# An attention and expert kernel with its first pair, its first plan and its hand-over in another order

## The chip, the cores and the metric

The kernel runs on one core of one Trainium2 chip. The metric is the device time of one execution in microseconds (us); lower is better. The engines are named as in the profile: PE (TensorE matmuls, PEld its weight loads), DVE (VectorE), ACT (ScalarE), POOL (GpSimd), SP (SyncE, which issues most DMAs). On-chip memory is SBUF; matmul results land in PSUM.

## The reference

Attention over 8 batches and 8 heads (sequence 576, head dimension 64), then a mixture of experts with one expert per token. All of it is float32.

```python
def _attn_ref(q, k, v):                       # 8, 8, 576, 64
    ...
    q_rot, k_rot = (rotate(q), rotate(k))     # rotary embedding by cos, sin of the position
    scores = scale * np.matmul(q_rot, k_rot.transpose(0, 1, 3, 2))
    scores = scores - np.max(scores, axis=-1, keepdims=True)
    attn = np.exp(scores)
    attn = attn / (np.sum(attn, axis=-1, keepdims=True) + 1e-09)
    return np.matmul(attn, v)

def _moe_ref(x, modality_id, w_gate, modality_bias, w1, w2):
    N, D, E, F = 4608, 512, 8, 1024           # tokens, width, experts, hidden
    logits = x @ w_gate + modality_bias[modality_id]
    e_idx = np.argmax(logits, axis=1)
    ...                                       # gate_w: the softmax value of that expert
    for e in range(E):
        mask = e_idx == e
        h = np.maximum(x[mask] @ w1[e], 0.0)
        out[mask] = gate_w[mask, None] * (h @ w2[e])
```

## The kernel before

**Attention.** The 64 heads are worked on as 32 pairs; pair n holds two heads of batch n // 4. One tile holds a pair's rotated queries and keys, 128 rows by 1216 columns. A step (called a part in the code) rotates such a tile: part 0 multiplies by the cosines (L230), part 1 by the sines (L232), part 2 adds (L234), part 3 copies the sum rounded to the matmul's type on ScalarE (`acopy`, shown as L221, `HL<-ST`: the "high" half) and part 4 subtracts to get the rest (L238, the "low" half). Two DMAs per pair (L246, `SW<-HL`) swap the two heads' rows. Parts 0, 1, 2 and 4 run on VectorE for pairs 0 and 1 and on GpSimd from pair 2 on. Pair 0's tile is done in three column ranges, `FIRST`, whose inputs and tables come by DMAs of their own (L154 to L156), each with all five parts before the next.

A pair's scores are made in nine units of 128 queries (L261), numbered 0 to 8; unit 8 holds the last 64 queries of both heads. Units go through a ring of three PSUM tiles. Each gets a minimum on VectorE (L270; the sign of the scores is turned) and an exponential on ScalarE with the row sums (L277). Then P is transposed on PE through the same ring (L283, six "fills": F0 to F3, FA, FB), each evacuated half by VectorE (L315) and half by ScalarE (L221, `PH<-ps`, `PD<-ps`). AV matmuls (L339) in two halves A and B, copies, transposes back and division (L373 to L390) follow, and the finished rows go to the array X in DRAM.

**Routing and plans.** After the last pair of a batch that batch's logits, chosen experts and ranks are worked out (`route`, thirteen steps), and five indirect DMAs from GpSimd's queue (`scatter`, L472) write its tokens' numbers and weights to a table, TAB, sorted by expert. A block is 256 tokens of one expert. The first plan (`plan(0)`) cuts 8 full blocks out of the first six batches, while the last two are still in attention; the second cuts the rest. A plan is a chain of operations on a single partition, rows of 8, 64 or 8 by 8 numbers. In `plan(0)` GpSimd does all but a shift (L492) and three reductions, which VectorE does.

**Expert blocks.** `m_plan` reads a block's expert and place into registers of SP; `m_ix` loads its two index lists from TAB; `m_gather` (L614) fetches its token rows by indirect DMAs, eight of them; `m_load1` and `m_load2` load the expert's weights into the staging tiles ST1 and ST2 (the same tiles that hold the attention's inputs and tables). The weights are split into a high part (ScalarE, L221, `W1H`, `W2H`) and a low part (VectorE, L218, `W1L`, `W2L`). `m_tr` (L655) transposes the gathered rows, `m_tre` splits them. `m_l1` is the first layer (L673), `m_l1e` its activation (L681, L682), `m_l2` the second (L690) with its scaled result `y` and the indirect DMA to the output (L694).

**What sets the order.** Every step of a pair has a key time in the table `KEYS`, in microseconds on a period of 14.438; step s of pair n stands at key(s) + 14.438 n. A second table, `AT`, gives the keys of routing, plans, scatters and of the first expert block. All are sorted by key and emitted in that order, and each engine works through its instructions in the order in which they were emitted; SP's DMAs keep theirs too. The work on the first expert block is keyed relative to pair 31, the last one, so that it lies among the last pairs' work; negative keys lie before that pair. When the last pair's step keys are used up, the attention's pools are closed, and only then are the tiles for the split second-layer weights opened.

## Time and profile before

| what | value |
|---|---|
| time, median of 3 runs | 974.46 us (974.25 to 976.87) |
| the profiled execution's own time | 978.22 us |
| its span from first to last instruction | 976.4 us |
| PE busy | 908.2 us, 93% of the span |
| VectorE busy | 674.2 us, 69% |
| ScalarE busy | 632.3 us, 65% |
| GpSimd busy | 663.8 us, 68% |

Times inside the trace are counted from the start of the span. The program has three stretches: the start, until pair 0's scores run; 32 pairs of attention, a pair being counted from its first score matmul to that of the next; and the expert blocks to the end. In the view by windows each row is one stretch, with its length, then for PE, PEld, DVE, ACT and POOL the busy time and in brackets the number of instructions, then the clock that PE was granted (1.00 is full), the DMA engines' mean share and GB/s. In a timeline row stand start, duration, engine, line, operation, output and inputs, and in square brackets how long the engine had been idle and what released it. PE is the busiest engine, but in the start and around the hand-over to the experts it waits; these places are read by window and not from the shares above.

### The profile page before, as it was taken

The page shows a single profiled execution, that of the slowest core. Times are in us where ns is not written, and L with a number is a line of the kernel's source. Part 1 is how long each engine was busy: PE and PEld are TensorE (multiplying, and loading weights), DVE is VectorE, ACT ScalarE, POOL GpSimd, SP SyncE. Part 2 cuts the span into 40 slices and gives each one's busy share as a digit, 9 for nine tenths or more (in the row PEclk, how much of TensorE's full clock was granted, in tenths as well). Part 3 has the DMA queues.
Part 4 walks back from the last instruction along what each step waited for, and adds up shares of the span by engine and source line. Part 5 has one row for each costly group of instructions (what it writes and reads, how often), then busy time and mean ns, then how long its engine had stood idle before and what let it go on. Part 6 is the DMA issues. An engine that isn't in the chain of part 4 may idle for free. (4 is left out here: it accounts for less than half of the span.)

```text
span 976.4 us, 24969 instructions
## 1 busy us (share of the span) xinstructions
PE 908.2 (93%) x9248; PEld 742.4 (76%) x9248; DVE 674.2 (69%) x1158; ACT 632.3 (65%) x1299; POOL 663.8 (68%) x498
## 2 busy tenths in 40 slices
PE   1899999999999999989977899999999999999996
PEld 1677677777777767767646689999998888899995
DVE  6677777787777777777754478677666666666771
ACT  1778787787787877868753355666555656556661
POOL 7776788889878798799656076557666666556500
PEclk9799999999999999999989899999999999999998
DMA  9645667566574755746751261111431611611100
GB/s 285 194 142 173 180 198 221 148 188 202 174 225 134 201 185 175 228 130 182 207 149 34 64 211 36 55 48 58 142 120 42 218 38 45 227 44 49 41 24 15
DMA packets 71964, 132.71 MB, mean 136 GB/s; under 512 B 28395, under 2 KB 48267, under 8 KB 66844
## 3 DMA queue, kind: packets, MB, share of 16 engines
q1 hardware_dynamic: 61436, 110.32, 37.8%
q0 software_dynamic: 9536, 19.48, 6.4%
q8 instruction: 75, 1.23, 0.6%
q10 hardware_dynamic: 864, 1.25, 0.4%
q14 instruction: 53, 0.43, 0.2%
HBM read 140.59 MB, written 19.77 MB: 164 GB/s over the span
## 5 line engine op out<-in xcount | busy, mean ns | idle before, releaser
L270 DVE TENSOR_REDUCE mn<-ps 128x1 f32<-128x576 f32 x288 | 205.4, 744 | 104.2 <-PE ps L261 67.3
L277 ACT ACTIVATE P<-ps,mn 128x576 f32<-128x576 f32 x288 | 210.4, 737 | 97.6 <-DVE mn L270 90.4
L614 POOL DMA_INDIRECT XG<-X,iy x152 | 180.9, 1190 | 47.5 <-issue 41.4
L673 PE MATMUL psH<-HL,W1H 128*128 128x256 f32 x1152 | 202.7, 279 | 0.0
L261 PE MATMUL ps<-HL 64*128 64x288 f32 x960 | 170.7, 315 | 29.8 <-ACT HL L221 14.9
L261 PE MATMUL ps<-SW 64*128 64x288 f32 x960 | 170.3, 316 | 9.0 <-DMA SW<-HL 4.7
L261 PEld LDWEIGHTS ps<-HL 64*128 64x128 f32 x960 | 137.7, 190 | 53.2 <-ACT P L277 15.9
L673 PEld LDWEIGHTS psH<-HL,W1H 128*128 128x128 f32 x1152 | 176.8, 188 | 1.7
L673 PE MATMUL psH<-HL,W1L 128*128 128x256 f32 x576 | 160.8, 279 | 0.7 <-DVE W1L L218 0.7
L261 PEld LDWEIGHTS ps<-SW 64*128 64x128 f32 x960 | 135.4, 190 | 24.4 <-ACT P L277 14.1
L218 DVE TENSOR_TENSOR W1L<-ST,W1H 128x1024 fp32r<-128x1024 f32 x76 | 90.0, 1222 | 84.6 <-ACT W1H L221 82.6
L339 PE MATMUL pa<-PH,V 128*64 128x320 f32 (+1 forms) x1024 | 142.2, 420 | 1.1 <-PE ps L261 0.7
L694 POOL DMA_INDIRECT out_dram<-y,ix x38 | 39.1, 1030 | 143.6 <-ACT y L693 129.8
L690 PE MATMUL psY<-W2H,SW 128*128 128x512 f32 x304 | 120.3, 396 | 1.4 <-ACT W2H L221 1.4
L690 PE MATMUL psY<-W2L,SW 128*128 128x512 f32 x304 | 120.4, 396 | 0.4 <-DVE W2L L218 0.4
L283 PE MATMUL ps<-idf,P 64*128 64x64 f32 x2624 | 105.3, 229 | 8.8 <-DVE PH L315 2.4
L283 PEld LDWEIGHTS ps<-idf,P 64*128 64x128 f32 x2624 | 92.6, 141 | 22.7 <-ACT PH L221 8.6
L315 DVE COPY PH<-ps 128x512 f32<-128x512 f32 (+1 forms) x160 | 97.3, 632 | 17.4 <-PE ps L283 10.9
L339 PEld LDWEIGHTS pa<-PH,V 128*64 128x64 f32 x1024 | 69.8, 139 | 51.5 <-issue 14.5
L673 PEld LDWEIGHTS psH<-HL,W1L 128*128 128x128 f32 x576 | 108.2, 188 | 0.9 <-DVE W1L L218 0.9
L221 ACT ACTIVATE PH<-ps 128x512 f32<-128x512 f32 (+1 forms) x160 | 84.0, 556 | 22.1 <-PE ps L283 14.9
L218 DVE TENSOR_TENSOR W2L<-ST,W2H 128x1024 fp32r<-128x1024 f32 x76 | 92.4, 1220 | 4.1 <-ACT W2H L221 3.6
(159 smaller groups left out, 1602.9 us busy)
## 6 DMA issues: line engine op xcount, KB each, us to landing
ST<-in_moe_w_dram SPq DMA_DIRECT2D x152, 512.0 KB
ST<-in_qk_dram SPq DMA_DIRECT2D x31, 1216.0 KB
SW<-HL SPq DMA_DIRECT2D x124, 232.0 KB
V<-in_v_dram SPq DMA_DIRECT2D x64, 128.0 KB
X<-X SPq DMA_DIRECT2D x8, 1024.0 KB
XG<-X,iy POOLq DMA_INDIRECT x152
V<-in_v_dram SPq DMA_DIRECT2D x64, 16.0 KB
X<-XT SPq DMA_DIRECT2D x32, 32.0 KB
```

The lines of the kernel that those rows point to most:

```text
L218: nc.vector.tensor_tensor(o, a, b, op=ALU.subtract)
L221: return nc.scalar.activation(o, i, AF.Copy, scale=scale)
L261: free(nc.tensor.matmul(ps[:, g, 0:288], t[:, wq, q0:q0 + P], t[:, wk, k0:k0 + 288], start=(m == 0), stop=(m == len(L) - 1)), seen)
L270: lastmin[d["ring", u]] = nc.vector.tensor_reduce(mn, d["S", u][:, :, 0:288], op=ALU.min, axis=AX.XY).ins
L277: nc.scalar.activation(p.rearrange("p (a b) -> p a b", a=2), ps[:, :, 0:288], AF.Exp, bias=d.pop(("m", u)), scale=-1.0, accum_out=d["sum"] ...
L283: free(nc.tensor.transpose(ps[0][:, g, c:c + 64], src[r, k0:k0 + P], idf[r, r]), ps[1])
L315: mine.append((nc.vector.tensor_copy if g else acopy)(o, i).ins)
L339: nc.tensor.matmul(pa[hh * 64:hh * 64 + 64, 0:c1 - c0], d["V"][:, hh, kt, :], r, start=(kt == 0), stop=(kt == 4))
L614: nc.gpsimd.indirect_dma_start(out=XG[s % 2][:, t, g, :], out_offset=None, in_=X.rearrange("n (i f) -> (n i) f", f=P)[0:rows], in_offset=b ...
L673: nc.tensor.matmul(ps[:, i, :], w[:, c, f0:f0 + P], x[:, c, :], start=(m == 0), stop=(m == 11))
L690: nc.tensor.matmul(ps, hx[:, c, t * P:(t + 1) * P], w[:, c, :], start=(m == 0), stop=(m == 23))
L694: nc.gpsimd.indirect_dma_start(out=out, out_offset=bass.IndirectOffsetOnAxis(ap=d["ix"][:, t, 0:1], axis=0), in_=y, in_offset=None, bounds ...
```

## The change

1. **Pair 0.** The column ranges are other ones: 288 key columns, then 544 that hold the last query block and the other keys, then the 384 in between. The parts of the ranges are interleaved (a part of the next range stands before the low half of the one before). The load for pair 1 is issued after the second range's swap and no longer with the first inputs. The units of pair 0 come as 8, 6, 7, 0, 1 to 5 in the nine places of the key table; its evacuations stand right behind their fills, and both its AV halves right after the last fill.
2. **Pair 1.** Its parts 0, 1, 2 and 4 run on GpSimd instead of VectorE; its high copy and low half stand after pair 0's last fill. Parts 0 to 2 of pair 2 follow right behind it on GpSimd. The load for pair 3 and the seven GpSimd operations of `setup2` (routing constants) come later.
3. **First plan.** All 24 operations are on VectorE, spaced by 1.0 in the key table instead of 1.5. The scatters are spaced by 2.5 instead of 9.0 or 10.5; they, the first index copies and the last two batches' scatters are declared independent of each other, so none waits for another's write to TAB.
4. **First expert blocks.** Index copies, gathers, weight loads, the first layer's weight splits and the transposes have earlier keys: block 0's index copy at -45 instead of -16.5, its gathers from -41 to -15.8 instead of -12.5 to -3.4, block 1's from -13.5, block 2's from -3, the splits at -20, -15, -11, -4 instead of -14, -9, -5, -1, the transposes in pair 30 instead of pair 31.
5. **Second-layer weights.** Their high part takes the place in SBUF of the P tiles, their low part that of the transposed P, each as soon as the last reader in pair 31 is done; the splits get keys 10.2 to 20.5 within pair 31, and the first block's second layer stands 0.1 after the last pair's end instead of 2.0. The PSUM pools of the experts wait tile by tile.

```diff
 AT = dict(
-    pl=1.5,
-    sc=(10.5, 9.0),
...
+    pl=1.0,
+    sc=(2.5, 2.5),
...
-    FIRST = ((0, 416), (K1, QW), (416, K1))
+    FIRST = ((0, Q0), (672, QW), (Q0, 672))
...
     def rope_(n, part, c0=0, c1=QW):
         d = st[n]
-        e = nc.vector if n < 2 else nc.gpsimd
+        e = nc.vector if n < 1 else nc.gpsimd
...
+        for _b, x in placed:
+            tc.declare_no_dep(inst, x, reason="rows of other tokens")
...
     def plan(ph):
-
-        V_ = nc.vector if ph else nc.gpsimd
+        V_ = nc.vector
...
-    for n in range(2):
-        for c in FIRST if n == 0 else ((0, QW),):
-            for part in range(5):
-                rope_(n, part, *c)
-                if part > 2:
-                    swap(n, part - 3, *c)
-        load(n + 2)
+    for part, c in ((0, 0), (1, 0), (2, 0), (3, 0), (4, 0), (0, 1), (1, 1), (2, 1), (3, 1), (0, 2), (4, 1), (1, 2), (2, 2), (3, 2), (4, 2)):
+        rope_(0, part, *FIRST[c])
+        if part > 2:
+            swap(0, part - 3, *FIRST[c])
+        if (part, c) == (4, 1):
+            load(1)
+    load(2)
...
-    setup2()
+    for part in range(3):
+        rope_(1, part)
...
+    first = (8, 6, 7, 0, 1, 2, 3, 4, 5)
...
+    full = max(K[f] for f in K if f[0] in "SF") + 0.05
...
+    OV[0].update(AVA=full + 0.01, AVB=full + 0.02)
+    for i, nm in enumerate(("HI", "SWH", "LO", "SWL")):
+        OV[1][nm] = full + 0.03 * (i + 1) - PER
+    for i, nm in enumerate(("T1", "T2", "R")):
+        OV[2][nm] = full + 0.03 * (i + 5) - 2 * PER
+    J(full + 0.15, "load", 0, load, 3)
+    J(20.5, "setup2", 0, setup2)
...
+        if g == 0:
+            for i in range(2):
+                Z((A["hi2"], A["lo2"])[i][0] - 0.01, weights2, i)
+        Z(A["hi2"][g], m_hi, 1, g)
+        Z(A["lo2"][g], m_lo, 1, g)
...
-        Z(end + A["sp2"][g], m_split, 1, g)
     Z(end + A["l2"], m_l2, 0, 0)
...
     att.close()
-    mw = ctx.enter_context(tc.tile_pool(name="mw", bufs=1))
-    W2[0] = mw.tile([P, 8, DM], F32R, name="W2H")
-    W2[1] = mw.tile([P, 8, DM], F32R, name="W2L")
```

Three places show how the order moves. A row names line, operation, output, inputs and shape. The first is the end of pair 0 on ScalarE (HL0, HL1: rotated tiles of even and odd pairs; `re` and P4 to P3: the row sums of pair 0 and the exponentials of pair 1). Before:

```order
L221 ACTIVATE PD_115<-ps1_120 128x2x64
L221 ACTIVATE PH_114<-ps2_121 128x8x64
L221 ACTIVATE HL0_81<-ST1_73 128x1216
L354 ACTIVATE re_457<-sum_240,EPS_80 128x9
L277 ACTIVATE P4_113,sum_427<-ps0_119,mn_437 128x576
```

After:

```order
L234 ACTIVATE PD_113<-ps1_129 128x2x64
L234 ACTIVATE PH_127<-ps2_130 128x8x64
L234 ACTIVATE HL1_82<-ST2_74 128x1216
L234 ACTIVATE HL0_81<-ST1_73 128x1216
L367 ACTIVATE re_470<-sum_235,EPS_80 128x9
L290 ACTIVATE P4_112,sum_453<-ps0_128,mn_461 128x576
```

The high copy of pair 1 (HL1) now stands there too, and that of pair 2 (HL0) is still ahead of pair 1's first exponential. On GpSimd, after the DMA that clears TAB, the same place reads (ST1, ST2: inputs of even and odd pairs):

```order
L200 DMA TAB_64<-PH_114 128x648
L205 CAST MF_133<-MI_132 128x40
L209 TENSOR_TENSOR BI_134<-MF_133,MBB_135 128x320
L210 TENSOR_SCALAR MF_133<-MF_133 128x40
L211 TENSOR_TENSOR P0_109<-MF_133,MBB_135 128x320
```

and after the change:

```order
L213 DMA TAB_64<-PH_127 128x648
L243 TENSOR_TENSOR ST2_74<-ST2_74,ST1_73 128x1216
L245 TENSOR_TENSOR ST2_74<-ST2_74 128x1216
L247 TENSOR_TENSOR ST2_74<-ST2_74 128x1216
L251 TENSOR_TENSOR HL1_82<-ST2_74,HL1_82 128x1216
L243 TENSOR_TENSOR ST1_73<-ST1_73 128x1216
L245 TENSOR_TENSOR ST1_73<-ST1_73,ST2_74 128x1216
L247 TENSOR_TENSOR ST1_73<-ST1_73 128x1216
```

Between pair 1's high copy and pair 2's, ScalarE's rows above, GpSimd has pair 1's low half (L251) and pair 2's three parts (L243, L245, L247). The second place is VectorE in pair 26 (`mn`: a unit's minimum; `ni`, `nf`, `nb`, `t88`: the plan's rows). Before:

```order
L270 TENSOR_REDUCE mn_6964<-ps1_120 128x1
L270 TENSOR_REDUCE mn_6974<-ps2_121 128x1
L270 TENSOR_REDUCE mn_7000<-ps1_120 128x1
L492 TENSOR_SCALAR ni_6968<-ni_6968 1x8
L270 TENSOR_REDUCE mn_7014<-ps0_119 128x1
```

After:

```order
L283 TENSOR_REDUCE mn_6974<-ps1_129 128x1
L510 TENSOR_TENSOR nf_6979<-RUN_72,CF_70 1x8
L283 TENSOR_REDUCE mn_6984<-ps2_130 128x1
L512 TENSOR_SCALAR ni_6978<-nf_6979 1x8
L514 TENSOR_SCALAR ni_6978<-ni_6978 1x8
L283 TENSOR_REDUCE mn_7014<-ps1_129 128x1
L517 CAST nb_7027<-ni_6978 1x8
L283 TENSOR_REDUCE mn_7029<-ps0_128 128x1
```

Where one plan step stood between the minima there are now four, and so on through pairs 26 and 27. The third is VectorE's tail of the last pair (X, G, XT: finished attention rows and logits; HX: the first block's hidden layer). Before:

```order
L682 SCALAR_TENSOR_TENSOR HX_85<-ps1_120,SW0_83 128x512
L384 TENSOR_TENSOR X_7888<-pa_8957,ri_8918 128x8x32
L387 TENSOR_TENSOR G_139<-pa_8957,ri_8918 128x2x16
L218 TENSOR_TENSOR W2L_8980<-ST2_74,W2H_8979 128x1024 x4
L655 STREAM_TRANSPOSE XG1_76<-XG1_76 128x512 x2
```

After:

```order
L231 TENSOR_TENSOR W2L_8947<-ST2_74,W2H_8882 128x1024
L709 SCALAR_TENSOR_TENSOR HX_85<-ps1_129,SW0_83 128x512
L397 TENSOR_TENSOR X_8005<-pa_8987,ri_8949 128x8x32
L400 TENSOR_TENSOR G_147<-pa_8987,ri_8949 128x2x16
L682 STREAM_TRANSPOSE XG1_76<-XG1_76 128x512 x2
```

The four subtractions of the second layer's low weights no longer stand in a row behind the last pair's work but between its steps.

125 lines of the change are left out of this document (75 added, 50 removed).

## The prediction

> **What bounds the kernel now.** First the view by windows, edges at first score matmuls of pairs 0, 1, 2, 3, 26, 27, 28, 30, 31, at the first matmuls of the first expert block's two layers and of the second block, and at PE's end. Columns after the length: busy time and instructions of PE, PEld, DVE, ACT, POOL, PE's granted clock, DMA share, GB/s.
>
> ```profile
> 14.86:36.34 21.48, 13.48 (x142) 11.45 (x144) 15.83 (x19) 10.18 (x24) 17.67 (x11) 0.76 0.73 234
> 36.34:51.20 14.86, 14.49 (x209) 10.78 (x206) 10.54 (x22) 11.64 (x32) 10.44 (x4) 1.00 0.55 170
> 51.20:65.81 14.61, 14.45 (x209) 10.81 (x205) 10.90 (x24) 11.55 (x32) 10.96 (x6) 1.00 0.57 173
> 413.61:432.72 19.11, 15.91 (x209) 12.14 (x206) 14.04 (x27) 11.76 (x32) 15.99 (x16) 0.91 0.48 144
> 432.72:447.57 14.85, 14.64 (x203) 10.86 (x203) 11.14 (x26) 11.70 (x32) 13.59 (x17) 1.00 0.71 156
> 478.26:496.07 17.81, 15.27 (x210) 10.98 (x206) 13.27 (x26) 13.42 (x32) 7.12 (x7) 1.00 0.59 161
> 496.07:524.15 28.08, 19.35 (x203) 13.38 (x203) 17.22 (x30) 15.32 (x36) 17.11 (x17) 0.82 0.44 124
> 524.15:550.96 26.81, 21.55 (x158) 16.47 (x157) 5.63 (x17) 5.28 (x12) 10.31 (x11) 0.87 0.12 21
> 550.96:562.88 11.92, 11.53 (x48) 9.02 (x49) 8.91 (x11) 7.47 (x10) 1.02 (x1) 1.00 0.37 123
> 562.88:968.00 405.12, 403.89 (x2599) 363.95 (x2597) 275.29 (x316) 236.29 (x287) 231.21 (x193) 1.00 0.26 85
> ```
>
> An ordinary pair (third row) takes 14.61 us with PE busy for 14.45: PE sets its length, VectorE has 3.7 us to spare. So do the expert blocks from the second on (last row). The change touches neither; it touches the rows where PE is not full: pair 0, pair 26 (19.11 at a clock of 0.91), pair 31 and the first block.
>
> **The start.** Timeline rows of before, with the chain that sets pair 0:
>
> ```profile
> 10.03 0.46 DVE L238 TENSOR_TENSOR HL<-ST,HL 128x288 fp32r<-128x288 f32 x1 [0.51 <-ACT HL L221]
> 14.84 0.69 DVE L238 TENSOR_TENSOR HL<-ST,HL 128x512 fp32r<-128x512 f32 x1 [0.69 <-ACT HL L221]
> 18.42 0.60 PE L261 MATMUL ps<-SW 64*128 64x288 f32 x1 [2.96 <-DMA SW<-HL]
> 23.16 2.07 DVE L270 TENSOR_REDUCE mn<-ps 128x1 f32<-128x576 f32 x3
> 36.62 0.59 ACT L221 ACTIVATE PH<-ps 128x512 f32<-128x512 f32 x1
> 37.10 1.22 ACT L221 ACTIVATE HL<-ST 128x1216 fp32r<-128x1216 f32 x1
> 38.41 0.74 ACT L277 ACTIVATE P<-ps,mn 128x576 f32<-128x576 f32 x1
> ...
> L261 PE MATMUL ps<-HL 64*128 64x288 f32 x960 | 170.7, 315 | 29.8 <-ACT HL L221 14.9
> L261 PE MATMUL ps<-SW 64*128 64x288 f32 x960 | 170.3, 316 | 9.0 <-DMA SW<-HL 4.7
> ...
> L238 POOL TENSOR_TENSOR HL<-ST,HL 128x1216 fp32r<-128x1216 f32 x30 | 83.4, 2781 | 7.7 <-ACT HL L221 7.5
> ```
>
> The second row ends at 15.53, its swap lands 2.9 us later (18.42), and only then do the scores of pair 0 run on: unit 8 stands first and has its queries in the third range (its products of high halves start at 14.86, those with swapped rows wait). After the change, unit 8 has all its columns when two ranges are through. The second low half would then end near 11.85: 10.49 for its counterpart today, plus 1.4 for 256 more columns in each of four VectorE parts (0.69 for 512 in the second row, so 0.345 each). Scores run at 11.85 + 2.9 = 14.75, 3.7 us sooner. A unit costs PE 1.2 us ((170.7 + 170.3) / 288), so the third minimum, which ends at 25.23 today, can end 14.75 + 3 x 1.2 + 0.74 = 19.1: today VectorE does pair 1's four full-width parts in between, and these leave it. If the rest follows at today's pace, pair 0's last evacuation ends at 31.1 in place of 37.2: 6.1 gained.
>
> Then the new order takes it back. ScalarE does pair 1's high copy, 1.22, until 32.3; next in its order stands the high copy of pair 2, which needs pair 2's finished sum. GpSimd can begin pair 1's low half only when pair 1's high copy is done, and pair 2's three parts stand behind that low half. Four operations of 2.78 us are 11.1: ScalarE would stand until 43.4, copy until 44.6, and reach pair 1's first exponential at about 44.9 against 38.41 today. What queues behind it are all nine exponentials of pair 1; three units' scores can be made ahead, then the ring is full and PE waits too.
>
> From that exponential to pair 2's first scores go 12.8 us today (51.20 - 38.41). The AV of pair 0 is part of these; by the rows below it is 5.6 us of PE, and it would be done already. So pair 2 starts between 44.9 + 7.2 = 52.1 and 44.9 + 12.8 = 57.7, against 51.20. ScalarE has 10.4 us of pair 1's work left from there (11.64 in the second window row, less a high copy), which puts it at 55.3, and that I take: **+4**. Bounds: -6, if GpSimd's parts were done in the shade and all of the gain kept, and +7.
>
> ```profile
> L339 PE MATMUL pa<-PH,V 128*64 128x320 f32 x16 | 2.4, 439 | 0.0
> L339 PE MATMUL pa<-PH,V 128*64 128x256 f32 x16 | 1.9, 385 | 0.0
> L339 PE MATMUL pa<-PD,V 128*64 128x320 f32 x4 | 0.7, 432 | 0.0
> L339 PE MATMUL pa<-PD,V 128*64 128x256 f32 x4 | 0.6, 379 | 0.0
> ```
>
> **The first plan on VectorE.** The trace shows what one VectorE plan operation costs beside GpSimd (timeline rows of pair 26; then minimum, median and maximum ns of L492's two executions):
>
> ```profile
> 420.67 2.75 POOL L238 TENSOR_TENSOR HL<-ST,HL 128x1216 fp32r<-128x1216 f32 x1
> 420.72 2.72 DVE L492 TENSOR_SCALAR ni<-ni 1x8 int32<-1x8 int32 x1 [0.76 <-POOL ni L490]
> 425.08 0.60 PE L261 MATMUL ps<-HL 64*128 64x288 f32 x1 [2.75 <-ACT P L277]
> ...
> L492 DVE TENSOR_SCALAR ni<-ni x2: 158/1439/2720, 420.7 to 596.7; 1x8 int32<-1x8 int32 x2
> ```
>
> Eight numbers take 0.158 us in one execution and 2.72 in the other, which begins 0.05 behind a GpSimd rotation operation and ends with it. The minimum behind it waits, the exponential behind that, and PE stands 2.75 in the third row and falls to half clock. So one hold of 2.7 us went to the pair's length in full, although VectorE has 3.7 to spare on average.
>
> The changed order puts 24 such operations, one per microsecond of key time, beside the eight rotation operations of pairs 26 and 27. A plan step due every microsecond should meet at least six of the eight, the others falling where VectorE is held up by the step before; a hold begins some time in the rotation's first microsecond or so and lasts for the rest, 2.0 us on average: 12. Add 1.7 for a stretch at half clock like pair 26's ((1 - 0.91) x 19.11), and take off what pairs 26 and 27 lose already, 19.11 + 14.85 - 2 x 14.61 = 4.7: **+9**. Bounds: nothing held, -4.7; all eight held to the full, 22.2 - 4.7 = +17.5.
>
> The Trainium skill (SBUF — State Buffer, "Who interferes with whom") says that VectorE's copies, casts and tensor-scalar operations in their faster modes, and its operations with two inputs in SBUF against a GpSimd operation that reads SBUF, wait for the whole GpSimd instruction, and that reductions never contend. The L492 row agrees with it for tensor-scalar operations; by it 20 of the 24 operations could be held, three of them casts, of which no row here shows one held. With the casts left out, 17 of 20 of the hold, 10.2, the sum would be 967.7.
>
> **The hand-over.** Waits in pair 31 and the first layer, by instruction and releaser (total, count, longest):
>
> ```profile
> PE ps L261 <- ACT P L277: 4.0, 1, 4.0
> PE ps L673 <- issue: 3.8, 6, 1.0
> PE ps L261 <- DVE XG L655: 2.4, 1, 2.4
> PE psY L690 <- ACT W2H L221: 1.4, 1, 1.4
> DVE XG L655 <- DMA XG<-X,iy: 5.2, 2, 3.4
> ```
>
> ```profile
> 497.17 0.99 POOL L614 DMA_INDIRECT XG<-X,iy  x1 [0.30 <-issue]
> 501.00 0.71 DVE L655 STREAM_TRANSPOSE XG<-XG 128x512 f32<-128x512 f32 x1 [1.76 <-DMA XG<-X,iy]
> ```
>
> The transposes wait in VectorE's order for block 0's last gathers, 5.2 us, pair 31's minima behind them and its scores behind those; PE's clock falls to 0.82. With the gathers 12 to 30 key microseconds sooner and the transposes in pair 30, that goes. From 496.07 to 550.96 are 54.89 us (28.08 + 26.81). What remains is an ordinary pair with half a weight split (1.2) left in it, 15.3, and the first layer with the rest of pair 31 at the work PE has there, 21.55 x 0.87 = 18.7 at full clock: 34.0, so -20.9. The second block's start gives 0.4 more (11.92 - 11.53).
>
> Against that stands GpSimd. In the 29 key microseconds from block 0's index copy to its last gather it has 29 / 14.44 x 11.1 = 22.5 of rotations and eight gathers of 1.19, 9.5: 32 in 29, and the last gather's rows land 2.8 us behind its end (498.16 to 501.00). I take half of the 3 us as lost, 1.5. And I take off 1.9, half of what the profiled execution lies above the median (978.22 - 974.46 = 3.76), because the "issue" waits may belong to it alone. Together **-18**. Bounds: -22 with neither of these two, and -10 if the transposes wait as they do now. Two of the four splits of the first layer's weights go from pair 30 to pair 29; since VectorE has 10.9 us of work in a pair and a split is 1.2 there, I leave both pairs at today's times, pair 30 at its 17.81.
>
> **Edits at nothing.** Groups of VectorE, ScalarE and GpSimd instructions (count, busy, mean ns, idle before):
>
> ```profile
> L218 DVE TENSOR_TENSOR W2L<-ST,W2H 128x1024 fp32r<-128x1024 f32 x76 | 92.4, 1220 | 4.1 <-ACT W2H L221 3.6
> ...
> L221 ACT ACTIVATE W2H<-ST 128x1024 fp32r<-128x1024 f32 x76 | 79.6, 1051 | 0.7 <-PE pa L370 0.7
> ...
> L472 POOL DMA_INDIRECT TAB<-VAL,oi x40 | 42.5, 1062 | 18.4 <-DMA TAB<-VAL,oi 7.7 <-issue 4.7 <-DMA ix<-TAB 2.0
> L614 POOL DMA_INDIRECT XG<-X,iy x152 | 180.9, 1190 | 47.5 <-issue 41.4
> ```
>
> The splits of the second layer's weights, four of 1.05 and four of 1.22, go under the first layer, where ScalarE and VectorE are busy for 5.28 and 5.63 of 26.81 us; without that cover PE stands the 1.4 of the W2H wait above, as today. The five scatters of a batch now stand close together: 5.3 us of GpSimd against its slack of 14.61 - 10.96 = 3.65 in a pair, so the next rotation is up to 1.7 late; its swap is needed a whole pair later. Without that cover the 1.7 would be paid in each of seven batches, 12 us. The waits for each other's writes that go (7.7 in the L472 row) were GpSimd's, which sets no end there. `setup2`, moved past the rotations of pairs 1 and 2, is needed first by routing after pair 3. PSUM waits by tile only relax.
>
> **Sum.** +4 + 9 - 18 = -5 on the profiled execution (978.22 to 973.2, span 976.4 to 971.4); taken off the median of 974.46 it is **969.5**.
>
> **The rivals.**
>
> *Plan steps are not held.* For it: the other L492 took 0.158, a plan step need not meet a rotation if GpSimd lags, and 24 steps of 0.2 are only 5 us in the slack of two pairs. Against it: the 2.72 row. The term is then -4.7 instead of +9: 955.8. Chance 0.22.
>
> *Every rotation is held for nearly all of its time.* The place is VectorE in pairs 26 and 27, the price 2.78 for each of the eight. The sum turns positive where the plan term passes 14, which is 17 us of hold beside the half clock: from the seventh whole rotation on. With all eight, 22.2 + 1.7 - 4.7 = +19, it is -18 + 4 + 19 = +5, 979.5, and 981 with a half-clock stretch in pair 27 too. For it: L492 was held for all but 0.05; against: VectorE's next steps need ScalarE or PE in between. Chance 0.13. This is the rival on the other side.
>
> *The gathers still come late.* GpSimd's order is the longer now, and a scatter, a gather or a held rotation (the 2.75 row works both ways) can push block 0's gathers into pair 31. The transposes wait as before, 5.2 and 3.4 of the gain remain lost: -9.4, 978. Chance 0.12.
>
> *ScalarE does not wait at the start* (the sum of pair 2 is ready because GpSimd begins early): start -6.1, 959.4. Chance 0.08. Against: the low half of pair 1 cannot begin ahead of its high copy.
>
> **How the numbers follow.** The forecast has 0.45 (963 to 976 as its own range, some 0.6 of it below 971.5). A measurement here tells 0.3%, 2.9 us, from no change. Faster: 0.27 of the forecast, 0.22 and 0.08 of the rivals, 0.57. Same: 0.14 of the forecast, 0.08 from the late gathers: 0.22. Slower: 0.04 of the forecast, 0.13, and the rest of the late gathers: 0.21. Low end 955 (plan steps not held), high end 981 (all held).
>
> **What would show it.** After the change, ScalarE should idle for some 11 us before pair 1's first exponential, released by GpSimd; if it does not, the start term is wrong. VectorE's plan steps should show 1 to 2.8 us beside GpSimd's rotations and some 0.16 elsewhere, and pairs 26 and 27 together some 43 us (29.2 + 13.7); 29 to 31 says that nothing is held. From pair 31's start to the second layer should be 34 to 38 us, with no wait for XG and none for W2H. Were pair 31 as long as before, the gathers were the wrong cause.

## The result and the profile after

The changed kernel takes 1002.13 us (median of 4 runs, 1000.68 to 1003.75) against 974.36 (974.19 to 976.87) before: a ratio of 1.0279 with a 95% interval of 1.0254 to 1.0305. It is 27.8 us slower. The prediction was 969.5 with a range up to 981; it had the wrong sign.

The profiled execution took 1001.04 us, its span is 999.2. The view by windows, with the columns and the edges of the prediction's first fence (edges here: pairs 0, 1, 2, 26, 27, 28, 29, 30, 31, first matmul of the second layer, PE's end):

```profile
11.23:42.31 31.08, 18.65 (x184) 14.42 (x184) 12.52 (x21) 11.37 (x28) 14.14 (x8) 1.00 0.53 158
42.31:63.19 20.88, 12.41 (x166) 10.92 (x164) 9.53 (x18) 10.92 (x28) 20.32 (x14) 0.67 0.59 194
63.19:428.98 365.79, 352.48 (x4888) 260.99 (x4886) 270.96 (x600) 281.70 (x745) 302.28 (x174) 1.00 0.63 184
428.98:450.56 21.58, 17.84 (x211) 13.30 (x207) 21.02 (x37) 12.15 (x33) 17.47 (x12) 0.80 0.51 130
450.56:472.95 22.39, 18.43 (x208) 12.99 (x205) 19.77 (x36) 11.74 (x30) 12.64 (x5) 0.81 0.37 113
472.95:487.56 14.61, 14.45 (x208) 10.82 (x204) 10.90 (x24) 11.55 (x32) 7.77 (x5) 1.00 0.38 94
487.56:508.87 21.31, 16.55 (x212) 12.53 (x210) 13.14 (x32) 13.18 (x35) 19.77 (x16) 0.87 0.80 232
508.87:535.66 26.79, 19.33 (x208) 13.96 (x206) 18.05 (x32) 16.02 (x38) 19.56 (x20) 0.75 0.80 190
535.66:574.10 38.44, 35.23 (x365) 28.38 (x361) 19.56 (x38) 19.36 (x43) 9.53 (x11) 0.93 0.09 19
574.10:989.97 415.87, 415.18 (x2648) 373.26 (x2646) 282.33 (x329) 240.63 (x293) 235.98 (x194) 1.00 0.27 86
```

The kernel before was profiled a second time among the experiments (its run is told below). Its rows for the same stretches, from pair 2 on:

```profile
50.52:416.51 365.99, 352.12 (x4890) 265.00 (x4887) 270.95 (x600) 283.08 (x745) 302.88 (x174) 0.99 0.64 183
416.51:435.80 19.29, 16.39 (x212) 12.05 (x207) 14.17 (x27) 11.75 (x32) 16.44 (x16) 0.91 0.54 170
435.80:450.56 14.76, 14.54 (x207) 10.84 (x204) 11.06 (x26) 11.70 (x32) 13.36 (x17) 1.00 0.70 135
450.56:465.16 14.60, 14.44 (x204) 10.82 (x203) 10.89 (x24) 11.55 (x32) 13.11 (x8) 1.00 0.62 195
465.16:480.76 15.60, 14.73 (x210) 10.95 (x209) 12.24 (x31) 12.26 (x35) 12.90 (x12) 1.00 0.61 183
480.76:497.78 17.02, 14.96 (x211) 10.97 (x206) 13.45 (x27) 13.66 (x34) 6.83 (x6) 1.00 0.61 164
497.78:545.38 47.60, 36.35 (x364) 28.12 (x360) 22.55 (x46) 20.20 (x46) 28.55 (x29) 0.93 0.35 88
545.38:961.89 416.51, 415.41 (x2646) 373.01 (x2646) 284.86 (x326) 243.57 (x296) 234.50 (x194) 1.00 0.27 86
```

Row by row the two give where the time went:

| stretch | before, first trace | before, second trace | changed | change against the second |
|---|---|---|---|---|
| span's start to pair 2 | 51.20 | 50.52 | 63.19 | +12.7 |
| pairs 2 to 25 | 362.4 | 366.0 | 365.8 | -0.2 |
| pairs 26 and 27 (first plan) | 34.0 | 34.1 | 44.0 | +9.9 |
| pair 28 | 15.1 | 14.6 | 14.6 | 0 |
| pair 29 | 15.6 | 15.6 | 21.3 | +5.7 |
| pair 30 | 17.8 | 17.0 | 26.8 | +9.8 |
| pair 31 to the second layer | 54.9 | 47.6 | 38.4 | -9.2 |
| from there to PE's end | 416.5 | 416.5 | 415.9 | -0.6 |

The sum is +28.1, and the medians differ by 27.8. Four places lose 38 us, and one gains 9. Such differences between two executions are good to a few us in a long stretch: pairs 2 to 25 took 362.4 to 370.5 in the traces of this case. The following rows show how the time went.

**The start.** Timeline rows of the changed kernel: SP's DMA issues, then PE, ScalarE and GpSimd.

```profile
14.06 0.58 SPq L153 DMA_DIRECT2D ST<-in_qk_dram  x1
14.74 2.99 SPq L259 DMA_DIRECT2D SW<-HL  x4
...
23.75 0.60 PE L274 MATMUL ps<-SW 64*128 64x288 f32 x1 [3.00 <-DMA SW<-HL]
...
37.67 2.76 POOL L251 TENSOR_TENSOR HL<-ST,HL 128x1216 fp32r<-128x1216 f32 x1 [6.41 <-ACT HL L234]
45.94 2.74 POOL L247 TENSOR_TENSOR ST<-ST 128x1216 f32<-128x1216 f32 x1
...
48.71 1.22 ACT L234 ACTIVATE HL<-ST 128x1216 fp32r<-128x1216 f32 x1 [11.12 <-POOL ST L247]
50.03 0.72 ACT L290 ACTIVATE P<-ps,mn 128x576 f32<-128x576 f32 x1
```

Pair 1's 1216 KB load is issued at 14.06, and the third range's swap stands behind it; the products that need the swapped rows begin at 23.75, six us after the issue of the swap ended (17.73). Pair 0's last evacuation ends at 36.50 on ScalarE and 37.05 on VectorE, only 0.7 sooner than before (37.21 and 37.72). Then comes the wait that the prediction named: ScalarE is idle for 11.12, released by pair 2's sum on GpSimd, and pair 1's first exponential starts at 50.03 instead of 38.41.

**The plan.** Timeline rows of pairs 26 and 27, GpSimd's rotation operations and VectorE's plan steps beside them:

```profile
435.36 2.78 POOL L251 TENSOR_TENSOR HL<-ST,HL 128x1216 fp32r<-128x1216 f32 x1
440.58 2.79 POOL L245 TENSOR_TENSOR ST<-ST,ST 128x1216 f32<-128x1216 f32 x1
449.43 2.77 POOL L243 TENSOR_TENSOR ST<-ST,ST 128x1216 f32<-128x1216 f32 x1 [1.00 <-DMA ST<-in_qk_dram]
...
435.28 2.89 DVE L517 CAST nb<-ni 1x8 f32<-1x8 int32 x1
440.11 3.32 DVE L532 TENSOR_SCALAR cmp<-cmp 1x64 f32<-1x64 f32 x1
449.87 2.35 DVE L548 TENSOR_TENSOR ch<-pes 1x8 f32<-1x8 f32 x1
452.26 0.16 DVE L550 TENSOR_SCALAR PLA<-ch 1x8 int32<-1x8 f32 x1
```

Each long step ends with the GpSimd operation beside it (435.28 + 2.89 = 438.17 against 435.36 + 2.78 = 438.14). Nine of the 24 take 0.96 to 3.32 us, 17.8 together; the others take 0.06 to 0.21. Not all of that reaches PE: over two ordinary pairs (29.2) the two pairs grew by 14.8, half of it idle time of PE and half (7.4) its busy time, 17.84 + 18.43 against 2 x 14.45, at clocks of 0.80 and 0.81.

**Pairs 29 and 30.** Timeline rows around pair 29's end (`OH` is the one-hot choice of experts in routing, which PE needs), and the groups of VectorE in pair 30's window:

```profile
501.36 2.76 POOL L245 TENSOR_TENSOR ST<-ST 128x1216 f32<-128x1216 f32 x1
504.68 0.22 POOL L452 TENSOR_SCALAR OH<-vv 64x8 bf16<-64x8 f32 x1
504.95 0.20 PE L463 MATMUL pa<-OH,UT 128*128 128x48 bf16 x1 [4.29 <-POOL OH L452]
```

```profile
L231 DVE TENSOR_TENSOR W1L<-ST,W1H 128x1024 fp32r<-128x1024 f32 x3 | 3.7, 1219 | 0.1
L231 DVE TENSOR_TENSOR HL<-XG,HL 128x512 fp32r<-128x512 f32 x2 | 2.2, 1104 | 1.1 <-ACT HL L234 1.1
L682 DVE STREAM_TRANSPOSE XG<-XG 128x512 f32<-128x512 f32 x2 | 1.4, 707 | 0.0
```

In pair 29 GpSimd is busy for 19.77 of 21.31 us, and PE stands 4.29 for a routing step of 0.22 us that is queued behind gathers and rotations. In pair 30 VectorE has 18.05 us of work: 3.7 + 2.2 + 1.4 = 7.3 of it is the first expert block's.

### The profile page after: what moved, and what is told of

It reads as the page before. It is cut to its first block, busy times and chain, and to the rows that moved or that the text cites. A ratio compares the mean times of both kernels' runs of the same rounds, so it can differ in the third digit from the quotient of the medians.

```text
span 999.2 us, 24938 instructions
## 1 busy us (share of the span) xinstructions
PE 920.6 (92%) x9248; PEld 751.6 (75%) x9248; DVE 684.2 (68%) x1174; ACT 631.7 (63%) x1299; POOL 670.7 (67%) x482
## 3 DMA queue, kind: packets, MB, share of 16 engines
HBM read 140.59 MB, written 19.77 MB: 160 GB/s over the span
## 5 line engine op out<-in xcount | busy, mean ns | idle before, releaser
L274 PE MATMUL ps<-HL 64*128 64x288 f32 x960 | 179.1, 323 | 22.0 <-ACT HL L234 11.2
L274 PE MATMUL ps<-SW 64*128 64x288 f32 x960 | 177.9, 323 | 21.3 <-DMA SW<-HL 11.0
L274 PEld LDWEIGHTS ps<-HL 64*128 64x128 f32 x960 | 141.9, 196 | 46.4 <-ACT P L290 20.0
L274 PEld LDWEIGHTS ps<-SW 64*128 64x128 f32 x960 | 139.7, 196 | 40.2 <-ACT P L290 23.4
L296 PE MATMUL ps<-idf,P 64*128 64x64 f32 x2624 | 108.1, 234 | 13.4 <-ACT P L290 5.8
L296 PEld LDWEIGHTS ps<-idf,P 64*128 64x128 f32 x2624 | 95.3, 145 | 27.7 <-ACT P L290 12.0
```

Source lines behind the costliest of these rows:

```text
L274: free(nc.tensor.matmul(ps[:, g, 0:288], t[:, wq, q0:q0 + P], t[:, wk, k0:k0 + 288], start=(m == 0), stop=(m == len(L) - 1)), seen)
L296: free(nc.tensor.transpose(ps[0][:, g, c:c + 64], src[r, k0:k0 + P], idf[r, r]), ps[1])
```

## The experiments

All edits are made to the changed kernel; the last run is the kernel before, unchanged. The first four kernels were run once each, on one chip, with the profiler on, where one such execution of the kernel before took 980.65; they are read by their windows. The others have a time of their own, as a ratio to the kernel before on the same chip. The start alone differs by some us between chips and between executions: with the start of before, pair 2 began at 48.9 to 52.8, and with the changed start at 63.2 to 66.3.

**The plan back on GpSimd.**

```diff
-        V_ = nc.vector
+        V_ = nc.vector if ph else nc.gpsimd
```

> The changed kernel with one line undone: the first plan's 20 operations that came to VectorE are on GpSimd again, at the changed spacing. Changed kernel for comparison: pairs 26 and 27 take 21.54 + 22.39 = 43.9 us (34.0 before), and in them nine plan steps on VectorE take 0.96 to 3.32 us instead of some 0.16. Theory (VectorE's steps are held by GpSimd's rotation operations): pairs 26 and 27 fall to 34 to 37, the time by 7 to 10, to 991 to 995. Rival (the two pairs are long because the scatters, now close together, push the rotations on GpSimd late): they stay above 41 and grow with the operations that GpSimd gets back; the time stays within 3 of 1002.

Pairs 26 and 27 take 18.54 + 16.66 = 35.2 us instead of 44.0 (windows of this run):

```profile
435.54:454.08 18.54, 14.86 (x210) 10.84 (x206) 14.09 (x28) 11.62 (x32) 16.11 (x17) 1.00 0.62 156
454.08:470.74 16.66, 15.22 (x209) 10.91 (x205) 11.04 (x25) 11.64 (x32) 15.30 (x19) 1.00 0.45 127
```

VectorE's busy time falls from 21.02 and 19.77 to 14.09 and 11.04. The theory's window holds, so the holds on VectorE are what the plan cost; the whole, 1017.5, does not, since this execution has something else in pair 30, which takes 42.76. The longest of PE's waits there:

```profile
PE ps L296 <- issue: 10.7, 16, 1.2
```

Sixteen waits of up to 1.2 us for nothing that the trace shows. They are taken up at the second profile of before.

**The gathers and transposes back.**

```diff
-    ix=(-45.0, -35.0, -13.5, 3.0),
-    rows=(-41.0, -13.5, -3.0),
-    gap=(3.6, 1.3, 1.3),
-    te=(-9.0, -8.4),
+    ix=(-16.5, -9.5, 4.0, 6.0),
+    rows=(-12.5, -5.5, 8.0),
+    gap=(1.3, 1.3, 1.3),
+    te=(-4.5, 0.7),
```

> The changed kernel with the index copies, the gathers and the transposes of the first expert blocks at their keys of before (index copy -16.5, gathers -12.5 to -3.4, transposes -5.0 and 0.2); weights and everything else as changed. Changed kernel: pairs 29 and 30 take 21.31 + 26.79 = 48.1 us (33.4 before), pair 31 to the second layer 38.4 (54.9 before). Theory (GpSimd, with the last rotations still to do, is overfull with gathers, and routing and rotations behind them come late): pairs 29 and 30 fall to 33 to 37; the transposes wait in pair 31 again, which gets 43 to 50; together 2 to 12 less than now. Rival (the pairs are long because of the first layer's weight splits, which were moved earlier, on ScalarE and VectorE): pairs 29 and 30 stay above 45, pair 31 gets longer all the same, and the time rises by 4 or more.

Windows of pairs 29 and 30:

```profile
489.64:505.22 15.58, 14.73 (x210) 10.94 (x209) 12.23 (x31) 12.52 (x35) 12.89 (x12) 1.00 0.74 209
505.22:534.62 29.40, 19.49 (x210) 13.19 (x206) 14.69 (x27) 14.11 (x33) 19.12 (x18) 0.80 0.82 179
```

Pair 29 is back at 15.58: its excess came from the gathers beside the rotations, and PE's wait for routing is gone. Pair 30 is not shorter, but unexplained waits stand in this execution too (3.2 us in pair 30), so it decides nothing there, nor does its time of 1016.3. The two pairs take 45.0, between the theory's 33 to 37 and the rival's, and pair 31 to the second layer took 52.2, above the theory's 43 to 50.

**The start of before.**

```diff
-    FIRST = ((0, Q0), (672, QW), (Q0, 672))
+    FIRST = ((0, 416), (K1, QW), (416, K1))
...
-        e = nc.vector if n < 1 else nc.gpsimd
+        e = nc.vector if n < 2 else nc.gpsimd
...
+    for n in range(2):
+        for c in FIRST if n == 0 else ((0, QW),):
+            for part in range(5):
+                rope_(n, part, *c)
...
```

> The changed kernel with the whole start of before: the three column ranges, their order, the units' order, pair 1's rotation on VectorE, the loads and the constants of routing where they were. Changed kernel: pair 2 starts at 63.19 (51.20 before). Theory (the start costs 12.0 and nothing later makes up for it or depends on it): pair 2 starts at 51.2, the later pairs are as in the changed kernel, the time falls by 11 to 13, to 989 to 991. Rival (the earlier loads and the GpSimd rotation of pair 1 also help later pairs, which would then be longer than the changed kernel's): the time falls by less than 8.

Pair 2 starts at 50.76, 12.4 sooner than in the changed kernel and 14 to 15.5 sooner than with the changed start on the same chip (66.26 and 64.84 in the two runs above), and pairs 2 to 25 take 366.2 against 365.8: nothing later makes up for the start or depends on it. The time of this execution, 1005.6 where the theory had 989 to 991, is again not to be read, since its pair 30 takes 35.2, with 5.4 us of waits that nothing explains.

**Pair 1's load first.**

```diff
         nc.scalar.dma_start(out=SIN[:, c0:c1], in_=rope[1, :, c0:c1])
+    load(1)
...
-        if (part, c) == (4, 1):
-            load(1)
```

> The changed kernel with one move undone: pair 1's load (1216 KB) is issued with the first inputs, as before, instead of between the second and the third range's swap. Changed kernel: the third range's swap is issued by 17.7 and its scores start at 23.75; pair 0's last evacuation ends at 37.05, ScalarE then stands 11.1, pair 1's first exponential starts at 50.03, pair 2 at 63.19. Theory (that load stands in the DMA queue ahead of the swap and delays it by some 5 us): the scores of the third range start at 18 to 20, pair 0's last evacuation ends at 31 to 33, ScalarE still stands some 11 for GpSimd, the exponential starts at 45 to 46 and pair 2 at 58 to 60; time 3 to 5 less. Rival (the load in front delays the first ranges' own loads by as much): the first scores come at 14 or later instead of 11.2, and pair 2 starts at 62 or later.

The theory fell: pair 2 starts at 66.03, no sooner than the 64.8 and 66.3 of the first two runs. The rival's reason is not the right one either, since the first scores start at 10.91. The timeline shows why:

```profile
10.78 0.56 DVE L244 TENSOR_TENSOR ST<-ST 128x384 f32<-128x384 f32 x1 [0.61 <-DMA ST<-in_rope_dram]
13.64 2.75 POOL L244 TENSOR_TENSOR ST<-ST,ST 128x1216 f32<-128x1216 f32 x1
13.84 2.96 DVE L246 TENSOR_TENSOR ST<-ST,ST 128x384 f32<-128x384 f32 x1 [1.87 <-DMA ST<-in_rope_dram]
16.83 3.02 DVE L248 TENSOR_TENSOR ST<-ST 128x384 f32<-128x384 f32 x1
20.44 2.43 DVE L252 TENSOR_TENSOR HL<-ST,HL 128x384 fp32r<-128x384 f32 x1 [0.59 <-ACT HL L235]
```

With its input there early, GpSimd begins pair 1's rotation at 13.64, while VectorE is still at pair 0's third range. Three VectorE operations of 0.56 us take 2.96, 3.02 and 2.43: 6.7 us lost to holds, where the load between the swaps had cost six. The third range's table also lands some 2 us later: that operation starts at 13.84, in the two runs above at 11.51 and 11.69. The later load of the changed kernel kept the two engines apart. So moving that one load to the front does not help. The execution took 1024.86, with 43.5 in pair 30 and 17.2 of it in unexplained waits of PE, so its time is not read either.

**The start mended in two places.**

```diff
-        if (part, c) == (4, 1):
+        if (part, c) == (4, 2):
             load(1)
...
+    for i, nm in enumerate(("HI", "SWH", "LO")):
+        OV[2][nm] = 14.0 + 0.1 * i - 2 * PER
```

> The changed kernel with two moves in its start: pair 1's load is issued behind the third range's swap instead of ahead of it, and pair 2's high copy on ScalarE stands behind the first three exponentials of pair 1 (key 14.0 instead of 10.05). Changed kernel: third range's scores from 23.75, ScalarE idle for 11.1 us ahead of pair 2's high copy, first exponential of pair 1 at 50.03, pair 2 from 63.19. Theory (the two waits are the start's loss, and they follow each other): third range's scores from 19 to 20, pair 0's last evacuation by 33, pair 1's first exponential at 43 to 45, pair 2 from 55 to 58; time 5 to 8 below the changed kernel, 994 to 997. Rival (the four GpSimd operations of 2.78 set the start whatever ScalarE does): pair 2 starts at 61 or later, time within 3 of 1002.

It takes 994.31 against 975.14 on the same chip, a ratio of 1.0210 (1.0171 to 1.0248): some 7 us below the changed kernel's 1.0279. Timeline rows of PE and ScalarE, and the window of pair 1, which ends at pair 2's start:

```profile
20.76 0.60 PE L274 MATMUL ps<-SW 64*128 64x288 f32 x1
...
43.99 0.74 ACT L290 ACTIVATE P<-ps,mn 128x576 f32<-128x576 f32 x1 [8.51 <-DVE mn L283]
```

```profile
39.63:57.53 17.90, 12.78 (x164) 11.18 (x163) 9.51 (x18) 10.73 (x27) 17.74 (x8) 0.71 0.63 201
```

The third range's products with swapped rows start at 20.76 with no wait for the swap, 7.5 us after pair 0's first score (13.28); in the changed kernel it was 12.5 (23.75 - 11.23). Pair 0's last evacuation on ScalarE ends 20.9 us after that first score instead of 25.3. So the load ahead of the swap is what held pair 0. Pair 1's first exponential starts at 43.99 and pair 2 at 57.53, both where the theory had them. What ends ScalarE's idle time is now a minimum, no longer GpSimd's sum. With the start of before the same chip showed 40.2 and 40.5 for that exponential, so some 3.6 us are left. They lie in pair 1's own chain: GpSimd is through the three parts at 32.55 and stands 2.81 for ScalarE's high copy; the low half ends at 38.12, and only then come its swap, the scores and the first minimum (43.20).

**Start and plan of before.** The edits of the first and the third experiment together (the plan's steps keep their changed spacing of 1.0).

> The changed kernel with the whole start of before and the first plan on GpSimd again. What stays changed: the scatters close together, the early gathers, transposes and weight splits, the places of the second layer's weights. Theory (the loss of 27.8 in the medians is 12.0 at the start, 10.0 in pairs 26 and 27, 14.7 in pairs 29 and 30, 3.4 in the other pairs, against 17 gained after pair 31's start): pair 2 starts at 51, pairs 26 and 27 take 34 to 37, pairs 29 and 30 together 45 or more; the time is 978 to 985, so still some 0.4 to 1% above before. Rival (pairs 29 and 30 are long because the plan and the start made everything late): these fall to 34 to 38 and the time to 962 to 968.

It takes 980.62 against 975.14 on that chip: 1.0049 (1.0019 to 1.0080). Of the 2.8% that the changed kernel loses, start and plan are 2.3 points; the rest of the change loses 0.5%. Windows of pairs 29 and 30 and from pair 31 to the second layer:

```profile
472.70:494.70 22.00, 16.48 (x211) 12.56 (x210) 12.93 (x32) 13.10 (x35) 20.46 (x16) 0.89 0.81 238
494.70:519.52 24.82, 18.01 (x209) 13.71 (x206) 20.00 (x32) 15.90 (x38) 19.40 (x20) 0.84 0.73 190
519.52:557.42 37.90, 34.57 (x365) 27.71 (x361) 19.58 (x38) 19.38 (x44) 10.54 (x11) 0.94 0.13 25
```

Pairs 29 and 30 stay long, without the late start and without the held plan: that is the hand-over's own doing.

**The transposes late.** Start and plan of before, and one line more:

```diff
-    te=(-9.0, -8.4),
+    te=(-4.5, 0.7),
```

> The kernel with start and plan undone (980.6 at 975.1 before; pair 29 22.0, pair 30 24.8, pair 31 to the second layer 37.9), and of the rest one thing moved: the first block's two transposes and the splits of its rows go from pair 30 to pair 31 (keys -5.0 and 0.2 for the transposes); gathers and weight splits stay early. Theory (pair 30 is long because VectorE has 20.0 us of work in it, 5 of it for the gathered rows): pair 30 falls to 17 to 20, pair 31 to the second layer gets 39 to 42 with no wait for the gathered rows, pair 29 stays at 21 to 22 with PE's 4.3 us wait for the routing step on GpSimd; time 975 to 979. Rival (pair 30 is long because of GpSimd and the swaps behind the weight loads): pair 30 stays above 23 and the time rises.

Pair 30 takes 20.54 instead of 24.82, with VectorE's work down from 20.00 to 16.78; pair 31 to the second layer 39.85 instead of 37.90; pair 29 stays at 21.44. The time is 979.57 against 976.78 (1.0012, 0.9985 to 1.0038); the interval overlaps that of the run before it, so the time alone does not tell the two apart. Of the two theories the one on VectorE's work is borne out, within its window for pair 31 and just above it for pair 30 and the time: PE's two waits for exponentials that stood behind the row splits (1.16 and 2.18 us) are gone. GpSimd's work in the pair fell too, from 19.40 to 16.23, so the run does not part the two engines fully, and 20.54 is still 3.5 above before.

**A spread hand-over.** Start and plan of before, and

```diff
+    ix=(-19.0, -16.5, 4.0, 6.0),
+    rows=(-14.5, -3.5, 8.0),
+    gap=(1.3, 1.3, 1.3),
+    te=(-5.5, 0.5),
+    hi=(-24.0, -20.0, -15.0, -11.0),
+    w1=(-29.3, -27.8, -24.5, -22.0),
```

> As the kernel with start and plan undone, and in addition the first block's hand-over spread anew: gathers of block 0 at -14.5 to -5.4 (behind the last rotation on GpSimd instead of beside it), the transposes at -6.0 and 0.0 (one in pair 30, one in pair 31, not both in pair 30), the first layer's weight splits at -24, -20, -15, -11 (two in pair 29, two in pair 30). Theory (pairs 29 and 30 are long because in pair 29 GpSimd has five gathers beside four rotation operations and routing, and in pair 30 VectorE has 18.05 us of work: 10.9 of its own, three splits of 1.2, two transposes and two splits of gathered rows): pairs 29 and 30 fall to 31 to 36, pair 31 to the second layer stays at 38 to 44, the time is 958 to 968, below both kernels. Rival (the weight loads' traffic is what lengthens pair 30, by making the swaps late): pairs 29 and 30 stay above 42, time 975 or more.

Pairs 29 and 30 fell to 19.05 and 17.85, just above the theory's window for the two, but pair 31 to the second layer rose to 48.67, and the time is 981.43 (1.0069, 1.0036 to 1.0101). The waits in pairs 30 and 31:

```profile
PE ps L275 <- DVE PD L329: 9.0, 1, 9.0
...
DVE XG L683 <- DMA XG<-X,iy: 6.2, 1, 6.2
```

The transpose waits for the gathered rows and PE behind it: the wait that the change had removed, at another place. Three of batch 6's scatters, now close together, stood between block 0's gathers on GpSimd (at 505.59, 510.52 and 514.48), one every 1.3 us or more.

**The spread hand-over again.** As before it, with

```diff
-    sc=(2.5, 2.5),
+    sc=(10.5, 9.0),
...
-    te=(-5.5, 0.5),
+    te=(-2.0, 3.0),
```

> The spread hand-over again (gathers of block 0 at -14.5 to -5.4, splits of the first layer's weights at -24 to -11, start and plan of before), with the two things mended that its trace showed: the last batches' scatters at their wide spacing again, so that only one stands among block 0's gathers, and the transposes at -2.5 and 2.5, behind the rows' arrival. In that trace VectorE stood 6.2 us for the gathered rows and PE 9.0 in pair 31. Theory (that wait is the whole of pair 31's excess): pairs 29 and 30 take 34 to 37 together, pair 31 to the second layer 38 to 41, the time is 965 to 971, 0.4 to 1% below before. Rival (GpSimd's gathers reach past the transposes wherever these stand, since it has eleven indirect DMAs of 1.3 us ahead of them): VectorE waits for the rows again and the time stays within 3 of before or above.

It takes 969.52 against 976.78 on the same chip: 0.9932 (0.9912 to 0.9952), 0.7% faster than before. Windows of pair 29, pair 30 and pair 31 to the second layer:

```profile
465.03:483.69 18.66, 16.18 (x211) 12.13 (x210) 14.08 (x33) 13.71 (x36) 12.91 (x12) 0.91 0.80 224
483.69:501.56 17.87, 15.48 (x209) 10.94 (x205) 15.18 (x27) 14.03 (x35) 12.06 (x10) 1.00 0.62 173
501.56:540.59 39.03, 35.33 (x362) 27.65 (x358) 21.80 (x42) 20.00 (x46) 23.12 (x24) 0.96 0.32 63
```

The three take 75.6 us; 80.2 in the second trace of before, 86.5 in the changed kernel. GpSimd's 23 us of gathers and scatters are in the last of these stretches now, where no rotation is left to do, and no VectorE instruction waits for them. The scatters and the transposes were moved at once, so the run does not say which of the two did more.

**The weights' places alone.** Start, plan, scatter spacing, gathers, transposes and first-layer splits of before; what stays is the second-layer weights' places and keys, earlier plan reads and weight loads, and the declarations that scatters and index copies don't wait for each other.

> Start, plan, scatter spacing, gathers, transposes and the first layer's splits at their places of before; what stays changed is the second-layer weights in the places of the attention's tiles with their splits inside pair 31, the second layer 0.1 after the last pair's end, the PSUM waits by tile, earlier weight loads and plan reads. Theory (most of the 17 gained in the hand-over comes from the early transposes): the time is 2 to 5 below before, 969 to 973; pair 31 to the second layer takes 50 to 53. Rival (it comes from the second layer's weights): it takes 38 to 42 and the time falls to 958 to 964.

The time is 972.33 against 975.14 (0.9981, 0.9946 to 1.0016): inside what can't be told from no change. Pair 31 to the second layer takes 40.95, which neither theory had with that time; pair 30 takes 21.80 instead of 17.0. PE stands 3.5 us there for a swap, until 490.76; the last swap issued ahead of that, at 482.66, stands right behind a weight load (481.47). In the second trace of before that wait is 1.3, in the changed kernel 1.7. So the rival of the spread run, weight loads that make a swap late, is seen here, and is small in the changed kernel. No VectorE wait for gathered rows stands in this run, with the gathers and transposes at their old keys: their earlier places were not needed for it. The runs do not say which of the parts left in it did that; one that bears on it is that GpSimd no longer waits for the scatters' writes or the index copy (5.5 us for `iy` in the second trace of before).

**Before, profiled again.** The kernel before, unchanged.

> The kernel before, unchanged, profiled again on this chip, so that the other runs of this call have a trace of before beside them. In the earlier trace: pair 2 from 51.20, pairs 2 to 28 take 411.4 us, pair 30 17.8, pair 31 to the second layer 54.9, with six waits of about 1 us that nothing explains inside the first layer (533 to 540). Theory (those waits belong to single profiled executions): they are at another place, or longer or shorter, and pair 31 to the second layer takes 48 to 52 without them. Rival (they belong to the kernel): the same six waits at the same place.

The execution took 973.08 us, 5.1 less than the one that the prediction was worked out from. From pair 31 to the second layer it needs 47.60 us instead of 54.89, just under the theory's 48 to 52, and from the first layer's start on PE has one wait:

```profile
PE psY L690 <- ACT W2H L221: 1.4, 1, 1.4
```

The six waits of about 1 us inside the first layer are gone. VectorE's waits for the gathered rows are there as in the first trace (8.2 us, 5.2 there). So what the first trace showed there as "issue" is no fixed part of the kernel.

## Why the prediction was wrong

**The start, predicted +4, measured +12.7 (12.0 against the trace that was shown).** The wait was forecast in the right place, with the right length (11.1, measured 11.12) and the right releaser. The step that failed is "if the rest follows at today's pace, pair 0's last evacuation ends at 31.1". It ended at 36.50, 5.4 later, and (counted from pair 0's first score) 4.4 of that went when the load was issued behind the third range's swap instead of ahead of it. That move was named in the change and costed nowhere: the DMA was not followed into the queue in which it now stands. The Trainium skill (DMA: Bandwidth & Descriptors, "Queues, rings and completion order") says that what one issuing engine sends is consumed in the order of its ring on each DMA engine; the trace agrees, with a load issued at 14.06 and the scores behind the next swap at 23.75, and so does the run with the load behind that swap. The other step is the way from the first exponential to pair 2. The prediction took 10.4 us between bounds of 7.2 and 12.8; it was 13.2 (63.19 - 50.03), above the upper bound, with PE at a clock of 0.67 in that window. That pair 0's AV was out of the way shows no gain there.

**The plan, predicted +9, measured +9.9.** The mechanism held, read from a single row of before, and pairs 26 and 27 took 44.0 where 43 was written. That the number is so close is luck in part, since two terms were off and made up for each other: six holds of 2.0 us, all of it PE's idle time, were expected, and nine of 17.8 in sum came, of which PE's idle time shows 7.4; and the low clock was put at 1.7 and cost 7.4 of PE's busy time. The Trainium skill (SBUF — State Buffer, "Who interferes with whom") says that casts too are among the operations that can contend; the row of L517, 2.89 us for a cast of eight numbers, agrees, and so do the two-input rows L548 and, in the run with the early load, L246.

**The hand-over, predicted -18, measured -9.8 where it was looked for and +15.5 just ahead of it.** Two steps failed. The first is the base: 54.89 us for pair 31 to the second layer. The prediction saw the unexplained waits and the 3.76 that the profiled execution lay above the median, and took off 1.9; the second trace is 7.3 shorter there. PE's idle time is 2.7 less in it, and its busy time 4.6 less (36.35 against 19.35 + 21.55, at a clock of 0.93 against 0.82 and 0.87). The changed kernel's 38.44 lies near the 37.4 that the prediction makes of it (34.0 + 1.5 + 1.9), with the waits for the gathered rows and for W2H gone as forecast, so against the trace that was shown the gain is nearly the forecast one, and against the second half of it. What the prediction gave as the reason, earlier gathers and transposes, is not shown: with the weights' places alone the wait went too, with both at their keys of before. The second step is "I leave both pairs at today's times". Pair 29 lost 5.7: GpSimd's 3 us of lateness were costed for the gathers alone, and not for what is queued behind them on that engine, routing steps that PE waits for. Pair 30 lost 9.8: its VectorE sum counted the splits of the weights that left it, and not the two transposes and two row splits that came in. With these, 10.9 + 3 x 1.2 + 2 x 0.71 + 2 x 1.1 gives 18 us for a pair of 14.6. Moving the transposes and row splits back shortened the pair by 4.3, in the kernel with start and plan undone. The sum alone does not give all of 26.8: PE's busy time grew by 4.4 too (19.33 against 14.96, at a clock of 0.75 against 1.00), and no run parts what else is in it.

**The edits at nothing.** Pairs 2 to 25 take about the same (366.0 and 365.8; on one chip 369.7 with the old spacing of the scatters and 370.5 with the new one), so the new spacing shows no cost above some 0.7 us there; beside block 0's gathers it put three scatters in their way (the spread run). The second-layer weights are ready in time, and the wait for W2H is gone, as forecast.

**The rivals.** "Every rotation is held for nearly all of its time" was on the right side, with 981, and the wrong place: the plan cost what the forecast said. "The gathers come late" did not happen; they came early, and others paid. No rival had the start or pairs 29 and 30 as the place of the loss. With 12.7 for the start and 15.5 for pairs 29 and 30 the prediction's sum would have been 12.7 + 9 + 15.5 - 18 = +19, and with the hand-over at -9.8 it is +27, which is what was measured.

## What to carry to other kernels

Work that is moved earlier to free a late stage lands in a stage that has its own sum: add up each engine's work there, all that comes and goes, before taking it at its old length. A DMA or a gather that moves is to be followed into its queue, and the question is what now stands behind it and who waits for that. And a gain that is read from one profiled execution is only as good as that execution: if it lies above the median of the runs, and shows waits that nothing explains, a second one is wanted before the term is sized. Here the unexplained waits in the first layer came to 3.8 us, and the stretch was 7.3 shorter without them.

## What the runs showed of the hardware

VectorE's operations on a handful of numbers and on 384 columns alike lasted until the GpSimd operation beside them was done, a cast of eight numbers 2.89 us where another took 0.15, and 384 columns up to 3.02 where 0.56 is usual; a reduction (L568, 0.20 us at 458.55, inside a GpSimd operation that ran from 458.19 to 460.94) did not, nor did an operation beside the same one that reads PSUM (L397, 0.41 us at 458.12). GpSimd's own operations were hardly longer for it: 2.75, 3.09 and 2.95 us beside the three held ones of the run with the early load, against 2.75 alone later in that run.

Single profiled executions showed stretches in which PE issued one instruction per microsecond or so with no wait that the trace names: 3.8 us in all in the first layer of the first trace of before, and 10.7, 3.2, 5.4 and 17.2 in pair 30 of the first four experiments, which ran on one chip; none in these places in the second trace of before, in the trace of the changed kernel or in the other six experiments. Gathers were being issued from GpSimd in each of them, but they were also issued where no such stretch occurred. The changed kernel and the run with the start mended have the same order in pair 30 as the run with the early load and show none there, so the order alone does not bring them on. Whether the chip or the single execution does was not tested, and what causes them was not found.
